# Storing only the sums of weights, and moving GpSimd's sums behind the chunk's operands

## The chip, the cores and the metric

One Trainium2 chip, one core. The time is the device time of one execution in microseconds (us), given as the median of the executions of a kernel with the lowest and the highest beside it. Engines are named as the profile names them: PE is TensorE, PEld its weight load, DVE VectorE, ACT ScalarE, POOL GpSimd, SP SyncE (SPq its DMA queue). SBUF holds the kernel's tiles, PSUM the banks (X, Y, acc) that the products are written to.

## The reference, cut to what matters

A Mamba-2 scan over chunks of tokens gives y; y, rearranged to 3072 rows of 256, goes through a merge of four experts.

```python
for c in range(nc):                       # chunks; the state is carried from one to the next
    ...
    y_intra = einsum(M, xc)
    y_inter = einsum(Cc, state) * exp(cum)
    y[:, :, sl] = y_intra + y_inter
    state = decay_full * state + sum(Bx)
...
x = y.transpose(0, 2, 1, 3).reshape(3072, 256)
for e in range(4):                        # w1[e]: 256 x 1024, w2[e]: 1024 x 256
    h = maximum(x @ w1[e], 0.0)
    out += p[:, e:e + 1] * (h @ w2[e])
```

All is fp32, and TensorE has most of the work: the two products of each expert.

## The kernel before

The tokens are taken in six blocks of 512. In each block the kernel walks through eight steps, a step being half of one expert's weights: step n = 8k + r uses the pieces w1(n) and w2(n), and n mod 8 says which piece it is. The products are done in a Strassen-Winograd form, with seven products where the plain form has eight. That needs the four blocks of a piece of weights (A11, A12, A21, A22) and sums of them (S1 to S4). GpSimd makes the sums once, in block 0, and writes each finished piece to DRAM; from step 8 on a piece is loaded from that copy. Steps 0 and 1 use the plain form, so their last sum, which overwrites A21, comes later ("part 1").

```python
PLAIN = 2
A11, S3, A12, A22, S1, S2, S4 = range(7)      # seven slots of a piece, S3 holds A21 at first
...
def load_w1(n):
    e, jj = divmod(n % SPB, JJ)
    t1 = wt1[n] = wts.tile([P, 7, HB], FP32, tag="wt1", name="wt1", bufs=5)
    if n >= SPB:
        nc.sync.dma_start(out=t1, in_=w1_d[n % SPB])          # from the copy
        return
    for k in range(2):
        nc.sync.dma_start(out=t1[:, 2 * k:2 * k + 2], in_=w1[e, k * P:k * P + P]...)   # cut
...
def sums_of(op, part):
    if part != 1:
        nc.gpsimd.tensor_add(op(S1), op(S3), op(A22))
        nc.gpsimd.tensor_sub(op(S2), op(S1), op(A11))
        nc.gpsimd.tensor_sub(op(S4), op(A12), op(S2))
    if part != 0:
        nc.gpsimd.tensor_sub(op(S3), op(A11), op(S3))

def sum_w1(n, part=None):
    if n < SPB:
        sums_of(lambda w: wt1[n][:, w]..., part)              # cut
        if part != 0:
            nc.gpsimd.dma_start(out=w1_d[n], in_=wt1[n])      # all seven slots
```

There are five buffers for w1 and five for w2. So the load of w1(5) has to wait until the piece w1(0) has been stored.

Beside the experts runs the scan of a later chunk, one part at a time. A chunk enters in an even step (`c_in`) and its output y is computed in an odd one (`c_out`). GpSimd makes two operands for it: MT after VectorE's second scan (`decay_part(c_in, 1)`) and cts after VectorE's dec scan (`decay_part(c_in, 2)`). In the loop, cut to the order of what the change touches:

```python
for n in range(PLAIN, NS):
    ...
    opened(n); total(n, 1, "11"); gated(n, "11", "z11")       # TensorE, ScalarE, VectorE
    for work in late:                                         # VectorE: two differences, carries
        work()
    if c_in is not None:
        masks(c_in)
        decay_part(c_in, 0)                                   # VectorE: first scan
    if n == PLAIN:                                            # GpSimd, from here
        for m in range(PLAIN):
            sum_w1(m, 1)
    elif n == PLAIN + 1:
        for m in range(1, PLAIN):
            sum_w2(m, 1)
    sum_w1(n + 2)
    if n > PLAIN:
        sum_w2(n + 1)                                         # GpSimd, to here
    ...
    if c_out is not None:
        outputs(c_out, ps_att, "att")                         # TensorE: y, needs cts and MT
    fmul(n, 5); fmul(n, 7); snap(n, 7)
    total(n, 7, "22")                                         # VectorE: frees bank Y
    ...
    if c_in is not None:
        decay_part(c_in, 1)                                   # VectorE scan, GpSimd MT
    fmul(n, 3)                                                # TensorE: bank Y again
    ...
    if c_in is not None:
        scores(c_in, ...); masked(c_in, (2, 3, 0, 1))         # TensorE, VectorE
    diff(n, "T3", "22", "12")
    if c_in is not None:
        decay_part(c_in, 2)                                   # VectorE dec scan, GpSimd cts
    smul(n - 1, 4)
    diff(n, "T1", "12", "11")
    ...
```

The instructions of each engine are issued in this order. The names in the profiles: a snap is ScalarE's copy of bank X; a total z is VectorE's sum of bank Y and a snap; a gate makes h from a bank or a total; a difference hT is one h less another; a carry passes the scan's state on to a later chunk.

## Time and profile before

| what | value |
|---|---|
| median of the first 3 executions | 657.55 us (656.83 to 658.2) |
| the profiled execution | 659.22 us, span 657.4 us, granted clock 0.994 |
| TensorE busy | 646.5 us of 657.4 |
| stores of pieces | 16 of 896 KB |
| loads from the copies | 80 of 896 KB |

From the profile's list of DMA issues (KB each, median us to landing), and the line of bytes:

```profile
wt<-w_d SPq DMA_DIRECT2D x80, 896.0 KB, 8.8
w_d<-wt POOLq DMA_DIRECT2D x16, 896.0 KB, 6.1
HBM read 108.18 MB, written 18.07 MB: 192 GB/s over the span
```

Bear in mind that the profiled execution was 1.7 us longer than the median. The rest of the profile is read in the prediction.

### The profile page before, as it was taken

The numbers are of one execution on the slowest core, as the hardware profiler recorded it, in microseconds if no ns is written. First come the engines' busy times: TensorE is split into PE (matmuls) and PEld (weight loads), VectorE is DVE, ScalarE is ACT, GpSimd is POOL, SyncE is SP. The second block draws the span as 40 slices with busy tenths as digits, with TensorE's granted clock in tenths as the row PEclk, the third lists the DMA queues.
The fourth block names the chain that finished last, engine by engine and source line by source line (L and its number), as shares of the span: only waits on it lengthen the run. The fifth ranks groups of instructions, "written<-read, shape, count | busy, mean of one in ns | idle before, by whom it ended". The sixth has DMA issues, their size and how long they took to land.

```text
span 657.4 us, 8922 instructions
## 1 busy us (share of the span) xinstructions
PE 646.5 (98%) x3367; PEld 543.1 (83%) x3367; DVE 483.3 (74%) x814; ACT 115.7 (18%) x247; POOL 109.6 (17%) x157
## 2 busy tenths in 40 slices
PE   7999979999999999999999999999999999999997
PEld 4788868888888888888888888888888888888886
DVE  8779867788686787876877868768767676756555
ACT  3111111221112122111122121112211212111110
POOL 4788382011000002000002000000100000100000
PEclk9999979999999999999999999999999999999999
DMA  7979998351867551576643467636076553156000
GB/s 237 322 302 349 329 368 328 138 221 29 268 210 277 193 185 58 190 247 242 218 183 135 127 226 261 209 155 225 24 246 208 201 202 129 57 170 214 0 1 32
DMA packets 68138, 126.83 MB, mean 193 GB/s; under 512 B 26600, under 2 KB 50048, under 8 KB 68096
## 3 DMA queue, kind: packets, MB, share of 16 engines
q1 hardware_dynamic: 65152, 111.10, 48.8%
q0 software_dynamic: 2304, 14.68, 5.6%
q8 instruction: 26, 0.43, 0.3%
q10 hardware_dynamic: 640, 0.49, 0.2%
q14 instruction: 16, 0.13, 0.1%
HBM read 108.18 MB, written 18.07 MB: 192 GB/s over the span
## 4 chain that ended last, share of the span: by engine, by line
PE 94%; DMA 3%; SPq 1%; POOL 0%; DVE 0%; issue 0%; ACT 0%; POOLq 0%
PE acc L534 41%; PE X L449 24%; PE Y L449 18%; PE g L366 2%; PE y L395 2%; PE acc L515 2%; PE y L389 1%; DMA wt<-in_w_dram 1%; PE X L498 1%; PE Y L498 1%; DMA wt<-w_d 1%; DMA xb<-in_xbc_dram 1%; SPq L146 0%; SPq L133 0%; PE a L309 0%
## 5 line engine op out<-in xcount | busy, mean ns | idle before, releaser
L461 DVE TENSOR_TENSOR z<-Y,snap 128x512 f32<-128x512 f32 x138 | 94.6, 686 | 131.4 <-ACT snap L456 85.9
L534 PE MATMUL acc<-hT,wt 128*128 128x256 f32 x736 | 183.4, 382 | 0.0
L456 ACT COPY snap<-X 128x512 f32<-128x512 f32 x138 | 80.8, 586 | 468.7 <-PE X L449 468.7
L534 PEld LDWEIGHTS acc<-hT,wt 128*128 128x128 f32 x736 | 138.8, 191 | 24.0 <-issue 6.0
L449 PE MATMUL X<-yS,wt 128*128 128x256 f32 x552 | 142.6, 381 | 0.0
L534 PE MATMUL acc<-h,wt 128*128 128x256 f32 x552 | 141.6, 379 | 0.0
L449 PEld LDWEIGHTS X<-yS,wt 128*128 128x128 f32 x552 | 105.6, 191 | 14.3
L534 PEld LDWEIGHTS acc<-h,wt 128*128 128x128 f32 x552 | 105.1, 190 | 14.1
L471 DVE SCALAR_TENSOR_TENSOR h<-z,gate 128x512 f32<-128x512 f32 x138 | 97.4, 706 | 3.5 <-PE acc L515 0.4
L449 PE MATMUL Y<-yT,wt 128*128 128x256 f32 x368 | 94.5, 379 | 0.0
L449 PEld LDWEIGHTS Y<-yT,wt 128*128 128x128 f32 x368 | 68.9, 190 | 10.6 <-DVE z L461 0.2
L478 DVE TENSOR_TENSOR hT<-h,hT 128x512 f32<-128x512 f32 x92 | 66.4, 722 | 1.6
L478 DVE TENSOR_TENSOR hT<-h,h 128x512 f32<-128x512 f32 x92 | 63.4, 713 | 0.8
L343 DVE TENSOR_TENSOR_SCAN LT<-ab,ident 128x512 f32<-128x512 f32 x42 | 52.6, 1254 | 0.1
L449 PE MATMUL Y<-yS,wt 128*128 128x256 f32 x184 | 50.3, 397 | 0.0
L348 POOL TENSOR_TENSOR MT<-xb,LT 128x128 f32<-128x128 f32 x20 | 8.6, 429 | 243.2 <-PE Y L449 125.4
L449 PE MATMUL X<-yT,wt 128*128 128x256 f32 x184 | 47.2, 379 | 0.0
L376 DVE TENSOR_TENSOR MT<-g,LT 128x256 f32<-128x256 f32 x96 | 33.9, 416 | 16.5 <-PE g L366 16.4
L329 POOL TENSOR_TENSOR cts<-ctm,dec 128x256 f32<-128x256 f32 x20 | 19.7, 984 | 155.5 <-ACT snap L456 155.4
L449 PEld LDWEIGHTS Y<-yS,wt 128*128 128x128 f32 x184 | 33.9, 193 | 8.4 <-issue 3.9
L471 DVE SCALAR_TENSOR_TENSOR h<-X,gate 128x512 f32<-128x512 f32 x50 | 34.3, 686 | 7.4 <-PE X L449 4.1
L449 PEld LDWEIGHTS X<-yT,wt 128*128 128x128 f32 x184 | 35.0, 190 | 4.7
(94 smaller groups left out, 336.4 us busy)
## 6 DMA issues: line engine op xcount, KB each, us to landing
wt<-w_d SPq DMA_DIRECT2D x80, 896.0 KB, 8.8
w_d<-wt POOLq DMA_DIRECT2D x16, 896.0 KB, 6.1
ab<-acut_d SPq DMA_DIRECT2D x21, 512.0 KB, 6.1
wt<-in_w_dram SPq DMA_DIRECT2D x32, 256.0 KB, 6.8
xb<-in_xbc_dram SPq DMA_DIRECT2D x24, 320.0 KB, 5.0
gate<-p_d SPq DMA_DIRECT2D x23, 256.0 KB, 8.3
out_dram<-ot SPq DMA_DIRECT2D x160, 16.0 KB, 4.7
ah<-ac_d SPq DMA_DIRECT2D x20, 64.0 KB
```

What stands on the lines that cost most here:

```text
L329: nc.gpsimd.tensor_mul(cts, s["ctm"], dec.unsqueeze(1).to_broadcast([HN, NT, P]))
L343: nc.vector.tensor_tensor_scan(out=LT[:, i * w:i * w + w], data0=s["a"][i], data1=ident.rearrange("p h s -> p (h s)")[:, :w], initial=0.0, ...
L366: nc.tensor.matmul(out=g.rearrange("p t s -> p (t s)"), lhsT=s["xb"][k, OBT:OBT + P], rhs=s["ctm"][k].rearrange("p t s -> p (t s)"), start ...
L376: nc.vector.tensor_mul(s["MT"][:, h, 0:P], s["g"][q], s["LT"][:, h])
L395: nc.tensor.matmul(out=y[32 * q:32 * q + 32, t, 0:w], lhsT=xb[:, h * D:h * D + D], rhs=MT[:, NT * q + t, 0:w], start=(first and t == 0), s ...
L449: nc.tensor.matmul(out=f[bank][:, j], lhsT=wt1[n][:, w, j * P:j * P + P], rhs=rhs, start=(i in (1, 2, 5) and j == 0), stop=(j == JJ - 1), ...
L456: nc.scalar.copy(out=s, in_=first[n]["X"])
L461: nc.vector.tensor_add(z, first[n]["Y"], first[n][i])
L471: nc.vector.scalar_tensor_tensor(out=h, in0=first[n][src], scalar=0.0, in1=g.unsqueeze(1).to_broadcast([P, JJ, HB]), op0=ALU.max, op1=ALU. ...
L478: nc.vector.tensor_sub(h[o], h[x], h[y])
L498: nc.tensor.matmul(out=f[bank][:, j], lhsT=wt1[n][:, w, j * P:j * P + P], rhs=yT[k][:, i, cols], start=(i == 0 and j == 0), stop=(i == 1), ...
L534: nc.tensor.matmul(out=acc[k, u][:, half], lhsT=w2_op(n, w)[:, j], rhs=rhs[:, j], start=(begins and j == 0), stop=(n % SPB == SPB - 1 and ...
```

## The change

Two changes go together. **First**, only the sums are stored in DRAM (4 of 7 blocks for w1; 5 of 7 for w2, because A11 and S3 lie interleaved there, so that A11 goes along); from step 8 on, the other blocks are loaded from the weights themselves. **Second**, GpSimd's sums stand at the end of a step, behind MT and cts of the chunk; two of the late last sums move ahead of the loop.

```diff
-    A11, S3, A12, A22, S1, S2, S4 = range(7)
+    A12, A22, A11, S3, S1, S2, S4 = range(7)
...
-    w1_d = [tc.dram_tile([P, 7, HB], ...)]
-    w2_d = [tc.dram_tile([P, 7 * HB], ...)]
+    w1_d = [tc.dram_tile([P, 4, HB], ...)]
+    w2_d = [tc.dram_tile([P, 5 * HB], ...)]
...
 def load_w1(n):
-        if n >= SPB:
-            nc.sync.dma_start(out=t1, in_=w1_d[n % SPB])
-            return
+        for k in range(2):                # A11 (and A21 in block 0), then A12 and A22
+            w = 2 - 2 * k
+            a_ = 2 if n < SPB or k else 1
+            nc.sync.dma_start(out=t1[:, w:w + a_], in_=w1[e, ...])      # cut
+        if n >= SPB:
+            nc.sync.dma_start(out=t1[:, S3:], in_=w1_d[n % SPB])
 ...                                      # load_w2 alike
-                nc.gpsimd.dma_start(out=w1_d[n], in_=wt1[n])
+                nc.gpsimd.dma_start(out=w1_d[n], in_=wt1[n][:, S3:])
-                nc.gpsimd.dma_start(out=w2_d[n], in_=wt2[n])
+                nc.gpsimd.dma_start(out=w2_d[n], in_=wt2[n][:, 2 * HB:])
...
     gated(1, "22", "Y")
+    sum_w1(0, 1)
+    sum_w1(1, 1)
     sum_w1(3)
...                                       # in the loop
             decay_part(c_in, 0)
-        if n == PLAIN:
-            for m in range(PLAIN):
-                sum_w1(m, 1)
-        elif n == PLAIN + 1:
-            for m in range(1, PLAIN):
-                sum_w2(m, 1)
-        sum_w1(n + 2)
-        if n > PLAIN:
-            sum_w2(n + 1)
...
         smul(n - 1, 4)
+        if n == PLAIN:
+            sum_w2(1, 1)
+        sum_w1(n + 2)
+        if n > PLAIN:
+            sum_w2(n + 1)
         diff(n, "T1", "12", "11")
```

More of the change, by code (lines that the diff above doesn't have):

```diff
@@ L96 @@
     p_d = tc.dram_tile([T // P, E, P], FP32, name="p_d")
-    w1_d = [tc.dram_tile([P, 7, HB], FP32, name=f"w1_d{i}") for i in range(SPB)]
-    w2_d = [tc.dram_tile([P, 7 * HB], FP32, name=f"w2_d{i}") for i in range(SPB)]
+    w1_d = [tc.dram_tile([P, 4, HB], FP32, name=f"w1_d{i}") for i in range(SPB)]
+    w2_d = [tc.dram_tile([P, 5 * HB], FP32, name=f"w2_d{i}") for i in range(SPB)]
     st = {}
@@ L128, in load_w1 @@
         t1 = wt1[n] = wts.tile([P, 7, HB], FP32, tag="wt1", name="wt1", bufs=5)
-        if n >= SPB:
-            nc.sync.dma_start(out=t1, in_=w1_d[n % SPB])
-            return
-        for k in range(2):
-            nc.sync.dma_start(
-                out=t1[:, 2 * k:2 * k + 2],
-                in_=w1[e, k * P:k * P + P].rearrange("p (a f) -> p a f", a=2)[
-                    :, :, jj * HB:jj * HB + HB])
+        for k in range(2):
+            w = 2 - 2 * k
+            a_ = 2 if n < SPB or k else 1
+            nc.sync.dma_start(
+                out=t1[:, w:w + a_],
+                in_=w1[e, k * P:k * P + P].rearrange("p (a f) -> p a f", a=2)[
+                    :, 0:a_, jj * HB:jj * HB + HB])
+        if n >= SPB:
+            nc.sync.dma_start(out=t1[:, S3:], in_=w1_d[n % SPB])
     def load_w2(n):
@@ L140, in load_w2 @@
         t2 = wt2[n] = wts.tile([P, 7 * HB], FP32, tag="wt2", name="wt2", bufs=5)
-        if n >= SPB:
-            nc.sync.dma_start(out=t2, in_=w2_d[n % SPB])
-            return
-        for i in range(2):
+        for i in range(2) if n < SPB else (1,):
             f = i * FH + jj * HB
             nc.sync.dma_start(
-                out=t2[:, i * 2 * HB:(i + 1) * 2 * HB].rearrange("p (j m) -> p j m", j=JJ),
+                out=t2[:, (1 - i) * 2 * HB:(2 - i) * 2 * HB].rearrange("p (j m) -> p j m", j=JJ),
                 in_=w2[e, f:f + HB].rearrange("(j p) m -> p j m", p=P))
+        if n >= SPB:
+            nc.sync.dma_start(out=t2[:, 2 * HB:], in_=w2_d[n % SPB])
     def w2_op(n, w):
```

## The prediction

> **What bounds the kernel now.** I read the page from the top: busy shares, the 40 slices, then the windows of single steps.
>
> ```profile
> PE 646.5 (98%) x3367; PEld 543.1 (83%) x3367; DVE 483.3 (74%) x814; ACT 115.7 (18%) x247; POOL 109.6 (17%) x157
> PE   7999979999999999999999999999999999999997
> PEclk9999979999999999999999999999999999999999
> ```
>
> TensorE (PE) is busy for 98% of the span, so only 657.4 - 646.5 = 10.9 us of it are idle. Of the few slices under 9, one lies inside the run: slice 6 (82 to 99 us), where the clock row dips as well. So I asked for the windows around it, one step of the main loop each (columns: length, busy us of each engine with its instructions, clock, DMA share, GB/s).
>
> ```profile
> 56.24:69.59 13.35, 13.35 (x75) 11.28 (x74) 13.09 (x17) 2.22 (x5) 11.65 (x16) 1.00 0.89 336
> 69.59:82.55 12.96, 12.96 (x66) 10.80 (x64) 10.54 (x21) 2.34 (x5) 2.51 (x4) 1.00 0.96 335
> 82.55:102.51 19.96, 16.61 (x76) 13.09 (x75) 14.08 (x18) 2.22 (x5) 17.76 (x25) 0.83 0.93 369
> 102.51:115.50 12.99, 12.99 (x66) 10.92 (x65) 10.29 (x19) 2.34 (x5) 0.75 (x2) 1.00 0.87 305
> 115.50:128.80 13.30, 13.30 (x76) 11.29 (x75) 9.08 (x18) 2.22 (x5) 1.02 (x1) 1.00 0.37 144
> ```
>
> These are steps n = 3 to 7. Odd ones write a chunk's output and take 13.35 and 13.30 us with PE never idle; n = 5 does the same work in 19.96. So one step holds a loss of 19.96 - 13.35 = 6.61 us; the others are pure TensorE time. The timelines of PE and GpSimd (POOL) give the cause (start, us, then the instructions).
>
> ```profile
> 86.00 1.03 PE L534 MATMUL acc<-h,wt 128*128 128x256 f32 x4
> 90.38 1.22 PE L389 MATMUL y<-cts,M 128*128 128x256 f32 x2 [3.35 <-POOL cts L329]
> 91.53 1.19 PE L395 MATMUL y<-MT,xb 128*32 128x144 f32 x16
> 92.65 2.08 PE L449 MATMUL Y<-yS,wt 128*128 128x256 f32 x4
> ...
> 98.19 1.03 PE L449 MATMUL Y<-yT,wt 128*128 128x256 f32 x4
> ```
>
> ```profile
> 80.25 1.21 POOL L160 TENSOR_TENSOR wt<-wt 128x256 f32<-128x256 f32 x1 [10.30 <-DMA wt<-in_w_dram]
> ...
> 88.31 0.57 POOL L178 DMA_DIRECT2D w_d<-wt  x1 [0.30 <-POOL wt L164]
> 88.90 0.74 POOL L348 TENSOR_TENSOR MT<-xb,LT 128x128 f32<-128x128 f32 x1
> 89.61 0.71 POOL L329 TENSOR_TENSOR cts<-ctm,dec 128x256 f32<-128x256 f32 x1
> ```
>
> PE waits 3.35 us for cts, the operand of chunk 6. GpSimd makes it only after the eight sums and two stores of w1(6) and w2(5), and these stood behind a load: GpSimd was idle 10.30 us until w1(6) had landed. After the wait, four matmuls take 2.08 us where they take 1.03 elsewhere. The load was late for its own reason, in the waits of SyncE's queue:
>
> ```profile
> SPq L133 <- DMA w_d<-wt: 19.1, 1, 19.1
> SPq L146 <- DMA w_d<-wt: 9.0, 1, 9.0
> ```
>
> The load of w1(5) waits 19.1 us until the store of w1(0), whose buffer it takes, has landed; w2(5) then waits 9.0 us for w2(0). All loads queue behind them, w1(6) being issued only at 68.23.
>
> **What the Trainium skill says.** "TensorE: Matmul & The Clock Gate", Part 1: the array's clock halves after an idle window of about 3.4 us and is released after about 3.4 us of activity, in free-running windows. The trace agrees: the gap is 3.35 us, then matmuls run at half rate, and the clock is full again by 98.19. The same page's table says that GpSimd's queue is strict FIFO: a sum waiting for a load holds cts behind it, as seen. "GPSIMD Engine Reference", section 1: its SBUF interface is shared with VectorE. The trace fits: VectorE's dec scan took 1.45 us at 84.22, beside GpSimd's sums, and 0.41 us at 57.48. "DMA: Bandwidth & Descriptors", specifications: line rate needs pieces of 512 B or more; the new loads have rows of 1 KB, so they should be only a little less efficient.
>
> **The change, part by part.**
>
> (a) Stores. 16 stores of 896 KB become 8 of 512 KB and 8 of 640 KB: 14.68 MB become 9.44, so 5.24 MB less. At the 335 to 370 GB/s of the windows above that is some 15 us of DMA time, all of it before about 115 us, where the queues are 87 to 96% busy. No matmul reads these copies until block 1, so it saves PE nothing directly; it makes the early loads land sooner.
>
> (b) Loads from step 8 on. The same seven blocks arrive, three of w1's and two of w2's from the weights in 1 KB rows, the rest from the copies: five DMAs instead of two for each of 40 steps, 120 more issues. At 0.3 to 0.6 us each (rows of SyncE's timeline) that is 1 to 2 us more of SyncE per 13.1 us step. In the waits of its queue it stands 230.2 us for PE to release w2 buffers, so it has that time. The data are ahead too: w1(13) was issued at 160.26 and its step starts near 194 us. DMA efficiency: at 66 to 78 us, mainly 1 KB rows, 317 GB/s went at a share of 0.905, 21.9 GB/s per engine; at 90 to 96 us, mainly long rows, 427 at 1.02, 26.2. 640 KB a step, 40 KB per engine, then take 1.83 instead of 1.53 us: 0.3 us of a 13.1 us step at a share near 0.5. Cost on the path: nothing.
>
> (c) Order on GpSimd. The final differences of w1(0) and w1(1) move ahead of w1(3)'s sums; in the loop a step's sums stand behind MT and cts of its chunk. Walking through with the durations seen (a sum 0.72, a store with its wait 0.9, a whole set of four and a store about 4.3 us): cts of chunk 4 ends at 38.4; w1(0), w1(1) until 41.7; w1(3), w2(3) until about 50.5; MT(5) once its scan is done, 52.5; the store of w2(0) near 54 (57.3 before); cts(5) as before at 58 to 59, its dec scan deciding; w2(1), w1(4) until 65 (PE needs them at 72); w1(5), w2(4) until 74 (needed in step 5, from 85 on). MT(6) at 79 behind its scan, cts(6) behind the dec scan that ended at 85.7 and, with GpSimd no longer beside it, should end near 84.2; so cts(6) is there at about 85.2 to 85.5. PE reaches y at 82.55 + (60.56 - 56.24) = 86.87. Then w1(6), w2(5) until about 94, needed at 95.9 + 2.6 = 98.5, and w1(7), w2(6) until 103, needed at 111. Every margin is positive; the smallest is cts(6)'s, about 1.5 us, as in later steps (cts done at 118.1, y near 119.75).
>
> (d) Sum. Removed from the path: the wait, 90.38 - 86.87 = 3.51 us (the modelled 3.35 plus matmul tail), and the slow clock after it: from y to the next Y<-yT 98.19 - 90.38 = 7.81 us instead of 65.27 - 60.56 = 4.71, so 3.10. Together 6.61, the step's excess found above. Added: nothing. 657.55 - 6.61 = 650.94. I add 0.3 for small new waits: 651.2 us, 1.0% less.
>
> **Rivals.**
> 1. VectorE takes the place of the wait. In step 3, with GpSimd busy 11.65 us beside it, it was busy 13.09 of 13.35 us; in step 5 it needed 14.08, and had the stall to hide in. Without the stall a lag of 0.7 us or so could reach PE, in step 5 or 6. Against it: step 3 ran so without any PE gap, and step 6 leaves it 2.7 us. It would make 651.5 to 652.5.
> 2. cts stays late, because moving the sums alone doesn't speed up what dec waits for, or GpSimd is still in the sums of w2(4) when MT(6) could start. By that page's window a wait under 2 us should leave the clock alone, giving 651.5 to 653; only one near 3.4 us gives the old 657.
> 3. More loads on SyncE's queue: a weight set or gate lands after its step starts. For: 8 output stores took 10.85 us to issue at 172.35, so the queue can block. Against: some 30 us of lead. It would cost a few us per block, 655 to 665.
> 4. The smaller stores alone were the cure and the order is idle: the same time, so it can't be seen in the total; running each half apart would.
>
> **Range and chances.** The floor is firm: PE's 646.5 us less the 3.1 of slow clock plus the 7.6 idle us that remain is 651.0. Below 649.8 nothing is left to gain; above, rivals 1 and 2 reach 653 and rival 3 more. Range 649.8 to 654. Faster by over 2% would be under 644.4, less than PE's own work with its start and end: 1%. Slower by over 2% needs rival 3 in every block: 2%. Within 2%: 97%.
>
> **What would show it.** Right: slice 6 without a dip in PE and clock; the odd step at about 13.3 us; no wait of PE for cts over 1 us; GpSimd's cts(6) ahead of the sums of w1(6); HBM written 12.8 MB (18.07 less 5.24), read as before; the steps after 120 us unchanged. Wrong: a new gap in PE's slices between 56 and 130 us whose releaser is VectorE, cts or a sum; or PE waiting for a wt DMA after 130 us.

## The result, and the profile after

The changed kernel took 653.75 us (653.67 to 654.51, 4 executions), the kernel before 657.31 us (656.83 to 658.2, 4 executions) beside it: 3.56 us less. The ratio is 0.9947, with a 95% interval of 0.993 to 0.9964. Ratios here are the mean time of one kernel's runs over that of the other's of the same rounds, so not quite the ratio of the medians quoted.

From the page of the changed kernel: its busy row, the PE and clock slices, and the bytes.

```profile
PE 642.9 (99%) x3367; PEld 541.2 (83%) x3367; DVE 482.8 (74%) x814; ACT 115.7 (18%) x247; POOL 110.7 (17%) x157
PE   7999999999999999999999999999999999999997
PEclk9999999999999999999999999999999999999999
HBM read 108.18 MB, written 12.83 MB: 186 GB/s over the span
```

The dip of slice 6 is gone in both rows, and 5.24 MB less are written, as worked out. The windows of steps 4, 5 and 6 (length, busy us of the engines, clock, DMA share, GB/s):

```profile
69.20:82.16 12.96, 12.96 (x65) 10.81 (x64) 11.48 (x21) 2.35 (x5) 3.75 (x5) 1.00 0.99 360
82.16:95.50 13.34, 13.34 (x75) 11.34 (x74) 11.51 (x17) 2.22 (x5) 10.64 (x13) 1.00 0.72 259
95.50:110.03 14.53, 13.20 (x65) 10.80 (x64) 13.50 (x19) 2.35 (x5) 7.77 (x10) 1.00 0.87 300
```

Step 5 has fallen from 19.96 to 13.34 us. But step 6 has become 14.53. Before, it took 12.93 us: the prediction's window of it, 12.99 us, ends at 115.50, but the first product of step 7 starts at 115.44. The timeline of PE shows the hole there, and that y of step 5 no longer waits:

```profile
86.48 0.59 PE L389 MATMUL y<-cts,M 128*128 128x256 f32 x2
...
101.55 1.89 PE L534 MATMUL acc<-hT,wt 128*128 128x256 f32 x8
104.77 1.13 PE L449 MATMUL Y<-yT,wt 128*128 128x256 f32 x4 [1.33 <-DVE z L461]
```

PE wants bank Y again and waits for the total z with which VectorE empties it. GpSimd's timeline in the changed kernel:

```profile
83.84 1.02 POOL L329 TENSOR_TENSOR cts<-ctm,dec 128x256 f32<-128x256 f32 x1 [4.64 <-ACT snap L456]
84.82 0.72 POOL L160 TENSOR_TENSOR wt<-wt 128x256 f32<-128x256 f32 x1
...
103.14 0.57 POOL L178 DMA_DIRECT2D w_d<-wt  x1 [0.30 <-POOL wt L164]
```

cts(6) is ready at 84.86, 1.6 us before PE asks. Then GpSimd sums with hardly a break; its last sum ends at 102.84 (0.30 us before the store shown), which is 7.3 us into step 6. In the kernel before the last sum ended at 101.99, before step 6 had begun. VectorE in step 6, before and then after: the pair of late differences (hT), the first scan (LT), and the total z.

```profile
105.84 1.41 DVE L478 TENSOR_TENSOR hT<-h,hT 128x512 f32<-128x512 f32 x2
...
107.90 1.22 DVE L343 TENSOR_TENSOR_SCAN LT<-ab,ident 128x512 f32<-128x512 f32 x1
109.37 0.69 DVE L461 TENSOR_TENSOR z<-Y,snap 128x512 f32<-128x512 f32 x1 [0.25 <-ACT snap L456]
```

```profile
98.91 2.66 DVE L478 TENSOR_TENSOR hT<-h,hT 128x512 f32<-128x512 f32 x2
...
102.92 1.21 DVE L343 TENSOR_TENSOR_SCAN LT<-ab,ident 128x512 f32<-128x512 f32 x1
104.05 0.66 DVE L461 TENSOR_TENSOR z<-Y,snap 128x512 f32<-128x512 f32 x1
```

Counted from the step's start, z comes at 109.37 - 102.51 = 6.86 us before and at 104.05 - 95.50 = 8.55 after. The pair alone has become 1.25 us longer, and two instructions of the carry behind it 0.7 us together. The scan, which starts when GpSimd has just ended, takes the same 1.2 us in both.

There is also a small gain that nobody asked for, in step 2. From that step's first matmul to step 3's it was 56.24 - 40.59 = 15.65 us before and 55.85 - 40.81 = 15.04 after. VectorE's second scan of chunk 5 explains it. The first fence is of before, where GpSimd was summing beside it; the second is of after, where GpSimd was idle from 50.13 to 51.95 (the sums of w1(4), which stood here before, now come at the step's end, and it waited for this very scan):

```profile
50.42 2.12 DVE L343 TENSOR_TENSOR_SCAN LT<-ab,ident 128x512 f32<-128x512 f32 x1
```

```profile
50.64 1.22 DVE L343 TENSOR_TENSOR_SCAN LT<-ab,ident 128x512 f32<-128x512 f32 x1
```

So the profiled spans balance: 657.4 - 652.0 = 5.4 us, made of 6.62 less in step 5, 0.61 less in step 2, 1.60 more in step 6, and a start that was 0.22 later. (The start is not the change's doing: the second profile of the kernel before, below, has it 0.20 later too.) But the medians differ by only 3.56. The rest has to be a matter of the executions compared, which the first experiment looks at.

### The profile page after: what moved, and what is told of

It reads as the page before. It is cut to its first block, busy times and chain, and to the rows that moved or that the text cites. A ratio compares the mean times of both kernels' runs of the same rounds, so it can differ in the third digit from the quotient of the medians. Undisturbed runs are those within 1.5% of the kernel's fastest.

```text
span 652.0 us, 9098 instructions
## 1 busy us (share of the span) xinstructions
PE 642.9 (99%) x3367; PEld 541.2 (83%) x3367; DVE 482.8 (74%) x814; ACT 115.7 (18%) x247; POOL 110.7 (17%) x157
## 3 DMA queue, kind: packets, MB, share of 16 engines
HBM read 108.18 MB, written 12.83 MB: 186 GB/s over the span
## 4 chain that ended last, share of the span: by engine, by line
PE 96%; DVE 2%; issue 1%; DMA 0%; POOL 0%; ACT 0%; SPq 0%; POOLq 0%; DVEq 0%
PE acc L534 42%; PE X L449 24%; PE Y L449 19%; PE g L366 2%; PE y L395 2%; PE acc L515 2%; PE y L389 1%; PE X L498 1%; PE Y L498 1%; DVE hT L478 1%; DMA xb<-in_xbc_dram 0%; DVE h L471 0%; PE a L309 0%; DVE LT L343 0%; DVE z L461 0%
```

## The experiments

The theory: (A) the change takes the wait for cts away, whose cost in before varies with the clock after it, and gives part back because GpSimd's sums, now later, slow VectorE where PE depends on it. Its rivals: the loss of before is constant; the smaller stores are the cure and not the order; the new gap comes from VectorE's own order or from the DMA traffic. Each kernel ran beside the kernel before on the same chip, and all gave the right result. Times are medians, lowest and highest in brackets.

| run | time, us | ratio to before |
|---|---|---|
| before_again | 657.01 (655.6 to 658.64) | 0.9998 |
| order_only | 653.88 (653.55 to 654.39) | 0.995 |
| dma_only | 654.13 (654.0 to 654.57) | 0.9954 |
| carry_late | 652.88 (652.71 to 653.25) | 0.9935 |
| filler | 656.33 (656.01 to 657.02) | 0.9985 |
| one_step | 655.27 (654.74 to 655.62) | 0.997 |
| early_w1 | 654.48 (654.2 to 655.14) | 0.9957 |
| dummy_sums | 655.62 (655.37 to 655.82) | 0.9976 |
| carry_scan_late | 669.57 (669.27 to 669.96) | 1.0188 |
| order_carry_scan | 669.82 (669.54 to 670.03) | 1.019 |
| dma_carry_scan | 676.04 (674.43 to 676.8) | 1.0282 |
| w2_late | 652.44 (652.1 to 653.05) | 0.9921 |

### before_again: is the loss of before always the same?

The kernel before, unchanged.

> The kernel before, unchanged, for the span and granted clock of each of its executions. Theory A: the profiled execution of before was an unlucky one. The wait of TensorE for cts in step 5 is always there (about 3.4 us), but the half-rate clock after it [...]varies from run to run: executions spread over 656.5 to 659.5 us, the shorter ones with the higher granted clock (0.997 to 0.998 against 0.994), median near 657.3. Theory B (rival): the loss is the same 6.6 us in every run, the clock is 0.994 each time, and the 659.22 of the profiled run is recording overhead.

Six executions spread over 3.0 us, where the changed kernel spreads over 0.8. The profiled one took 657.05 us, its span 655.3, with a clock of 0.996. Its PE timeline around the wait:

```profile
89.58 0.70 PE L389 MATMUL y<-cts,M 128*128 128x256 f32 x2 [2.55 <-POOL cts L329]
...
96.03 1.03 PE L449 MATMUL Y<-yT,wt 128*128 128x256 f32 x4
```

The wait is shorter than in the first profile (y starts 2.71 us late instead of 3.51), and from y to the next Y<-yT it takes 6.45 us instead of 7.81, where 4.71 is the undisturbed time. The loss is 2.71 + 1.74 = 4.45 us instead of 6.61, and that difference of 2.16 us is all but the whole difference of the two spans, 657.4 - 655.3. At half rate the time lost is half of the time that passes, so the slow stretch lasted about 6.2 us in the first profile and 3.5 us here (an estimate: twice 3.10 and twice 1.74). Theory A holds on that, though the executions reached a little lower (655.6) than it gave. The wait varies too, which A had not said.

The record has 37 executions of before in the rounds of these runs. The three with a granted clock of 1.00 took 656.17 to 656.24 us, the two with 0.994 took 659.03 and 660.80. Between these, clock and time do not keep one order (658.64 us came with 0.997, 657.63 with 0.996). So before is still 2.4 us over the changed kernel where no slow clock is recorded; the slow clock comes on top, and both parts vary.

### filler: what does the clock cost?

Idle products fill the wait of before. The edit, on before:

```diff
+        if n == 5:
+            turn(4)                       # four products of 512 columns, never read
         if c_out is not None:
             outputs(c_out, ps_att, "att")
```

> The kernel before with four idle products (512 columns each, about 0.86 us, 3.45 us in all, result never read) put into TensorE's stream just ahead of the output of chunk 6, where it waits for cts. Theory A: part of the loss of before is the half-rate clock after the wait. TensorE is kept busy through the wait, so the clock stays full and step 5 takes 13.35 + 3.5 = 16.8 us instead of 17.8 to 20.0; the time falls from 657.3 to 655.0 to 656.3 us although work was added, and the spread between runs falls to that of the changed kernel (under 1 us). Theory B: the slow products after the wait come from something else (their operands, the DMA load); the time stays at 657 or rises, and the products after the wait still take 2 us per four.

Measured 656.33, 0.03 us above what A gave. The window of step 5 in this run:

```profile
83.53:100.31 16.78, 16.78 (x84) 12.86 (x82) 13.69 (x18) 2.22 (x5) 15.16 (x20) 1.00 0.97 391
```

The clock is 1.00, and the step is as long as the products added: 13.35 + 3.43. More than 3 us of work were added and the kernel became 1.1 us faster than before (657.41 in these rounds; the interval of the ratio, 0.9971 to 0.9999, only just excludes no change). The executions spread over 1.0 us. The longest wait seen, 3.51 us, is hardly longer than the work added, so filling the wait alone could not gain 1.1 us: half-rate clock after the wait is a real part of before's loss. The usual loss follows as well, as an estimate: 3.43 + 1.08 = 4.5 us, as in the second profile of before.

### order_only and dma_only: which half of the change is the cure?

order_only is before with the second half of the diff, dma_only with the first.

> Before with the changed order on GpSimd only; stores of 896 KB and whole loads from the copies kept. Theory A: the order alone takes the wait for cts away, so the time is that of the changed kernel, 653.3 to 654.5 us, with the same new gap of TensorE of 1 to 2 us in step 6 behind VectorE. Theory B: the smaller stores are what brings the loads in time; with the order alone a wait for cts or for a sum of over 1 us stays and the time is 655 us or more.

> The changed kernel with the order on GpSimd of before; only the sums stored, the rest loaded from the weights. Theory A: the sums of w1(6) still stand ahead of cts(6), so TensorE still waits in step 5, though less, since the store of w1(0) lands sooner: a wait of 1 to 3 us, with or without the slow clock, 654 to 657 us. Theory B: the wait is gone and the time is 653 to 654 us.

order_only equals the changed kernel within 0.13 us, with the same gap of 1.33 us in step 6. dma_only came out at 654.13, within A's 654 to 657 us and 0.13 above B's. The time can't tell them apart, but the trace can: there is no wait for cts, where A gave one of 1 to 3 us, so A is wrong. GpSimd and then PE:

```profile
77.11 0.86 POOL L160 TENSOR_TENSOR wt<-wt 128x256 f32<-128x256 f32 x1 [6.36 <-DMA wt<-in_w_dram]
...
87.48 0.73 POOL L329 TENSOR_TENSOR cts<-ctm,dec 128x256 f32<-128x256 f32 x1
```

```profile
88.50 0.60 PE L389 MATMUL y<-cts,M 128*128 128x256 f32 x2
```

The smaller stores bring w1(6) about 2.5 to 3.1 us sooner (GpSimd starts on it at 77.11; at 79.56 and 80.25 in the two profiles of before). cts(6) is done at 88.21, and PE asks at 88.50. It is just in time, helped by a step 4 of 13.69 us instead of 12.96. That longer step is the price: GpSimd's sums of w1(6) now lie beside VectorE's second scan of step 4, which takes 1.74 us instead of 1.22 (at 79.24). Either half alone removes the wait, so they do not add up. Stores and loads were not run apart; but from step 8 on, where the new loads are, the steps of dma_only take the same 12.93 and 13.34 us as before, so the gain is put down to the stores.

### one_step: are the sums of step 4 the whole wait?

Before, with only step 4's `sum_w1(6)` and `sum_w2(5)` moved to the end of the step.

> Before with one thing alone: in step 4 the sums of w1(6) and w2(5) stand behind cts of chunk 6; stores, loads and all else on GpSimd as before. Theory A: these two sums ahead of cts were the whole wait; the time is 653.3 to 654.5 us as in the changed kernel, with a gap of TensorE of 1 to 2 us in step 6 since the sums of step 5 are pushed back beside VectorE there. Theory B: the early differences of w1(0) and w1(1) are needed too; a wait for cts of over 1 us stays, 655 us or more.

No wait for cts is left, so those two sets of sums were the wait. But 655.27 is 1.4 us more than order_only and above A's range. The trace places most of it: step 2 has kept its 15.66 us (0.6 of gain missing), and step 6 has become 15.01 instead of 14.53 us; my expectation had seen neither. In step 2 the slow scan (2.12 us, at 51.32) lies beside the sums of w1(4), which still stand ahead of MT here. The early differences of w1(0) and w1(1) alone would only swap places with other sums ahead of those, so the 0.6 us is most likely due to w1(4) going to the step's end; no run has either move alone.

### carry_late: VectorE's order in the gap

The carries of the states move behind the total that PE waits for.

```diff
         late = [two differences]
-        if PLAIN < n <= CPB: late.append(carry(n - 1))
-        if c_out is not None: late.append(carry(c_out))
+        carries = [the same two]
...
         total(n, 7, "22")
+        for work in carries: work()
```

> The changed kernel with the carries of the states (three VectorE instructions, 0.75 to 1.45 us) moved behind the total that frees bank Y for the next matmul. Theory A: the new gap of step 6 is VectorE's backlog, of which the carry is 1.4 us; taken out of the way, the gap of 1.33 us falls under 0.3 us and the time by 1.0 to 1.5 us, to 652.2 to 652.8. Theory B: the gap comes from somewhere else (ScalarE's snap or the scan); it stays above 1 us and the time stays at 653.5 to 654.5.

652.88, 0.87 us less than the changed kernel, a little short of the 1.0 to 1.5 given. No gap is listed; step 6 is 13.34 us, 1.19 less, and step 4 has lengthened from 12.96 to 13.29, which together make the 0.87.

### early_w1: take GpSimd away from step 6

The sums of w1(6) go into the time in step 4 when GpSimd is idle.

```diff
             decay_part(c_in, 0)
+        if n == 4: sum_w1(6)
...
-        sum_w1(n + 2)
+        if n != 4: sum_w1(n + 2)
```

> The changed kernel with the sums of w1(6) (4.4 us) moved in step 4 ahead of MT(6) and cts(6), into the 5.9 us in which GpSimd is idle there (the load has landed by then). Theory A: the gap of step 6 is VectorE slowed by GpSimd beside it; GpSimd then ends at about 99 instead of 103 us, the two differences of VectorE at 98.9 fall from 2.66 towards 1.41 us and the gap from 1.33 us to 0.4 or less: 652.4 to 653.2 us. Theory B: VectorE's order alone makes the gap; it stays above 1 us and the time at 653.5 to 654.5 us. It would be slower, 655 or more, if the load has not landed and GpSimd waits ahead of cts again.

The gap of step 6 went, and that step took 12.93 us. But the time rose to 654.48, a miss for A's number (and in the range of B, whose gap in step 6 did not stay): a gap of the same kind opened in step 4, which became 14.92 us instead of 12.96.

```profile
79.73 1.13 PE L449 MATMUL Y<-yT,wt 128*128 128x256 f32 x4 [1.72 <-DVE z L461]
```

GpSimd was now busy beside VectorE's late differences of step 4 (2.85 us a pair). The gap follows GpSimd's work: idle time of GpSimd in a step was not free time.

### dummy_sums: GpSimd's work alone, in a quiet step

The changed kernel with 22 subtractions whose result is never read, behind cts of step 12, where no sums are made.

```diff
+        if n == 12:
+            for _ in range(22):
+                nc.gpsimd.tensor_sub(a_cut, ident[0:96, 0:2], ident[0:96, 2:4])
```

> The changed kernel with 22 idle subtractions on GpSimd (256 columns, 96 partitions, result never read) behind the cts of step 12, where GpSimd otherwise has nothing to do; no DMA and no sum of weights is touched. Theory A: two-operand work on GpSimd slows VectorE's two-operand work, so in steps 13 and 14 the differences of VectorE go from 1.41 to 2.2 to 2.8 us a pair, and TensorE gets a gap of 0.5 to 1.6 us in step 14, like that of step 6: 654.2 to 655.4 us. Theory B: the lag of step 6 came from the DMA traffic or the loads of that stretch; VectorE's times in steps 13 and 14 stay as they are and the time at 653.8.

655.62 us, 1.87 more than the changed kernel and 0.2 over A's range. The same place of step 14 in the changed kernel and in this run (VectorE), then PE in this run:

```profile
205.52 1.41 DVE L478 TENSOR_TENSOR hT<-h,hT 128x512 f32<-128x512 f32 x2
```

```profile
205.32 2.35 DVE L478 TENSOR_TENSOR hT<-h,hT 128x512 f32<-128x512 f32 x2
...
208.55 1.75 DVE L343 TENSOR_TENSOR_SCAN LT<-ab,ident 128x512 f32<-128x512 f32 x1
210.22 0.66 DVE L461 TENSOR_TENSOR z<-Y,snap 128x512 f32<-128x512 f32 x1
```

```profile
210.94 1.13 PE L449 MATMUL Y<-yT,wt 128*128 128x256 f32 x4 [1.01 <-DVE z L461]
```

No DMA and no sum of weights was touched, and the same gap arises; step 14 takes 14.67 us instead of 12.93, which is nearly all of the 1.87. Note which lines are longer: those whose two inputs both lie in SBUF (hT, scan). z, with one input in PSUM, still takes 0.66, though GpSimd's work lasts until 214.35. The Trainium skill has this in "SBUF — State Buffer", "Who interferes with whom": a VectorE instruction with two SBUF inputs contends with a GpSimd instruction that reads SBUF. This run agrees, and the cause of the gap is shown.

### carry_scan_late, order_carry_scan, dma_carry_scan: one move too many

All three add to carry_late's edit that the first scan moves behind the same total: on the changed kernel, on order_only and on dma_only.

```diff
             masks(c_in)
-            decay_part(c_in, 0)
...
         for work in carries: work()
+        if c_in is not None: decay_part(c_in, 0)
```

> The changed kernel with the carries and the first scan of a chunk's decays both moved behind the total that frees bank Y. Theory A: in steps 4 and 6, 13.29 and 13.34 us with the late carries against 12.96 without any lag, the scan is what still stands ahead of that total; both steps fall to 13.0 us, no gap of TensorE stays behind the start, and the time is 652.0 to 652.6 us. Theory B: the scan is then late for the masked scores at the step's end or holds the output of the chunk; a new gap appears there and the time is 653 us or more.

> The same two moves on VectorE with the changed order on GpSimd alone, stores and loads as before. If the smaller stores and the loads from the weights are worth nothing on the path once the order is changed, this equals carry_scan_late within 0.4 us (652.0 to 652.8); if the loads' earlier landing matters, it is slower by 0.5 us or more.

> The same two moves on VectorE with the smaller stores alone, order on GpSimd as before. There cts(6) was ready at 88.21 us and TensorE asked at 88.50, after a step 4 of 13.69 us: just in time. Theory A: with VectorE's lag of step 4 gone TensorE asks up to 0.7 us sooner, and part of the gain comes back as a wait for cts of up to 0.7 us; 653.0 to 654.0 us, slower than carry_scan_late. Theory B: the order is worth nothing once the loads come sooner: within 0.3 us of carry_scan_late.

A was plainly wrong: 669.57 us. The scores of the entering chunk use banks X and Y at the step's end, which VectorE's gates and totals have to empty first. Both scans, with one gate between them, now stand ahead of the last of those:

```profile
191.69 0.70 PE L366 MATMUL g<-ctm,xb 32*128 32x256 f32 x4 [0.35 <-DVE h L471]
```

This and the pause after the first scores make each pair of steps 193.29 - 165.98 = 27.31 us, where the changed kernel has 188.84 - 162.57 = 26.27: 1.04 us in each of the 13 even steps from 8 to 32, which is 13.5 of the 15.8 us lost. The other six steps in which a chunk enters changed by -0.57 to 1.45 us. order_carry_scan comes within 0.25 us of carry_scan_late, so with the order changed the smaller stores and the loads from the weights bring nothing that these runs show. dma_carry_scan has, in step 4, a wait of 2.85 us for a gate and half-rate products after it; its own question, whether cts would be late, can't be told from that.

### w2_late: put the sums where VectorE has room

The sums of w2(6) move from the end of step 5 behind MT(7) in step 6.

```diff
             decay_part(c_in, 1)
+        if n == 6: sum_w2(6)
...
-        if n > PLAIN: sum_w2(n + 1)
+        if n > PLAIN and n != 5: sum_w2(n + 1)
```

> The changed kernel with the sums of w2(6) moved from the end of step 5 behind MT(7) in step 6, where GpSimd was idle from 107.1 to 111.7 us. Theory A: the gap of step 6 is VectorE slowed by GpSimd in the first 7 us of that step; GpSimd now ends its sums near 98.5, so the pair of differences at 98.9 takes 1.4 instead of 2.66 us, the gap goes, step 6 falls from 14.5 to 13.0 us and the time to 652.1 to 652.8 us. Theory B: GpSimd's work now falls on VectorE's dec scan and on cts(7), and PE waits 0.5 to 1.5 us for those in step 6 or 7 instead: 653.3 to 654.5 us.

652.44 us, as A had it, and better than both kernels: 0.9921 of before, 1.3 us less than the changed kernel. VectorE's pair, and the window of step 6:

```profile
99.07 1.41 DVE L478 TENSOR_TENSOR hT<-h,hT 128x512 f32<-128x512 f32 x2
```

```profile
95.65:108.58 12.93, 12.93 (x65) 10.85 (x64) 11.69 (x19) 2.35 (x5) 6.46 (x9) 1.00 0.89 273
```

No step from 3 to 7 now has an idle PE. What is left of idle time lies at the start and the end.

## Why the prediction was right or wrong

The measured 653.75 lies within 2% and in the range, but near its top and above the 653 that rivals 1 and 2 were said to reach; that the range held it was in part luck. The forecast was a fall of 6.4 us, though; it was 3.6. By its own steps:

**What bounds the kernel**: right. PE sets the time; the loss sat in step 5, and its chain (store, load, sums, cts, y) was as read.

**(a) Stores**: the bytes were right (written 12.83 MB). "It saves PE nothing directly; it makes the early loads land sooner" was right too, but the size of that was left open. It is 2.5 to 3.1 us for w1(6), by itself enough to take the wait away (dma_only). Rival 4 was thus nearly true of the stores, but not of the order: either half is enough.

**(b) Loads**: right, no cost on the path. order_only, without the new loads, is 0.13 us from the changed kernel, and order_carry_scan 0.25 from its partner.

**(c) Order on GpSimd**: the walk held within about 1.5 us; cts(6) was ready at 84.86 for a predicted 85.2 to 85.5. It checked only when each sum was needed by PE, never what GpSimd's later end does to VectorE. It did not see the 0.61 us of step 2 either, which is the same effect with the sign reversed.

**(d) Sum**: two terms failed. "Removed: 6.61" was measured in one execution that was 1.7 us longer than the median from which it was subtracted. The second profile of before lost 4.45. Its steps against those of the changed kernel, 4.46 less in step 5, 0.42 less in step 2 and 1.60 more in step 6, make 3.28 us, and the spans differ by 3.3. If the medians (3.56 apart) are to balance in the same way, the usual loss is 3.56 + 1.60 less the 0.42 to 0.61 of step 2, so 4.5 to 4.7 us (an estimate; filler gave 4.5 independently). "Added: nothing" was wrong: step 6 added 1.60 us. That step 2, unforeseen as well, gave 0.4 to 0.6 us back was luck.

**The floor**: "firm" at 651.0 was a slip. 646.5 - 3.1 + 7.6 is a span, and the time of an execution was 1.8 us longer than its span in both profiles (659.22 against 657.4, 653.8 against 652.0). In the time that was forecast the floor is 652.8, so the point forecast of 651.2 lay below what its own figures allow. w2_late, which also has the gain of step 2, took 652.44.

**Rivals**: rival 1 came true, in step 6, with 1.60 us where it gave 0.3 to 1.3. So did one of the prediction's own signs of being wrong: a new gap of PE between 56 and 130 us released by VectorE (1.33 us at 104.77, too short to show in the slices). All its signs of being right came too. The argument against it ("step 3 ran so without any PE gap, and step 6 leaves it 2.7 us") failed in its second half: those 2.7 us were step 6's room in a trace where GpSimd was all but idle in it (0.75 us busy). Step 3 also has no scan of an entering chunk. dummy_sums shows the mechanism, carry_late and w2_late take it away in two ways, and early_w1 moves it. Rivals 2 and 3 did not come. Rival 2's rule that only a wait near 3.4 us slows the clock did not hold: half rate followed a wait of 2.55 us in before_again.

What stays open: the wait itself varied between two profiles of before (3.51 and 2.71 us); the runs do not say why beyond the load's landing, 0.7 us apart. In what way the half-rate stretch depends on the wait was not tested. And no run has the smaller stores without the new loads, or the early differences without the other moves.

## What to carry to other kernels

Idle time of GpSimd is not free where VectorE works from SBUF beside it: when work is moved off one engine's path, ask which engine it now lies beside, and in which part of the step that engine is what PE waits for. Before a loss read in one trace is subtracted from a median, compare that execution's time with the median. Two cures of one wait do not add up, so test each half alone.

## What the Trainium skill lacked or had wrong

- "TensorE: Matmul & The Clock Gate" gives an idle window of about 3.4 us before the clock halves. Here recorded gaps of 2.55 us (before_again) and 2.85 us (dma_carry_scan) were followed by half-rate products, four in 2.08 us instead of 1.03; gaps of 1.33 and 1.72 us were not. (The ends of products are modelled in the profile, so the gaps are approximate.) In before_again the halving came late: the first products after the gap still ran at nearly full rate (y in 0.70 us, where it took 1.22 in the first profile and 0.59 without a wait).
- The same page says that the count of slow products at a kernel's start varies from run to run with the free-running window; it does not say so of a gap within a kernel. Here one wait with such a slow stretch made six executions of one kernel spread over 3.0 us (in part because the wait itself varied), and dma_carry_scan's four over 2.4, where all kernels without it spread over 0.4 to 1.0 us.
- "SBUF — State Buffer" has the rule on VectorE and GpSimd, but, apart from two single ratios, no size for long stretches of such work. Here a pair of two-input differences went from 1.41 to 2.35 to 2.85 us and a scan from 1.22 to 1.75 to 2.12 us, while GpSimd's own subtractions went from about 0.73 to 1.06 us.
